# A spectral layer with a gated feed-forward part: who folds which block in the first stage, Newton's steps in three operations, and a new order of the first stage

## The chip, the cores and the metric

The kernel runs on one core of one Trainium2 chip. The metric is the device time of one execution in microseconds (us); smaller is better. Before the change it is 432.95 us, the median of three executions.

## The reference

The input `x` is one sequence of S = 2048 rows of D = 512. A layernorm is followed by a two-dimensional FFT, a filter, and the inverse FFT; a second layernorm is followed by a gated feed-forward part of width F = 1376.

```
def _layernorm(x, axis=-1, eps=1e-5):
    m = jnp.mean(x, axis=axis, keepdims=True)
    v = jnp.var(x, axis=axis, keepdims=True)
    return (x - m) / jnp.sqrt(v + eps)

def _A_ref(x, w_r, w_i):
    X = jnp.fft.rfft2(x, axes=(-2, -1))
    X = X * (w_r + 1j * w_i)
    return jnp.fft.irfft2(X, s=(S, D), axes=(-2, -1))

def _B_ref(x, w_gate, w_up, w_down):
    h = gelu(x @ w_gate, approximate) * (x @ w_up)
    return h @ w_down

h = x + _A_ref(_layernorm(x), w_r, w_i)
out = h + _B_ref(_layernorm(h), w_gate, w_up, w_down)
```

## The kernel before

All transforms are matmuls on TensorE (PE). The first stage takes `x` in 16 blocks of 128 x 512, in the tile `gh`, which arrive in the order of their numbers, blocks 0 and 1 apart and then two at a time. The order of the work on each engine is written out by hand, in the list `START`: a letter is a step, a number its block or group, and each engine gets its instructions in the order of the list. The steps of the first stage are:

- `s` and `g`: statistics of a block. For the blocks in `BY_SCALAR` ScalarE (ACT) does both, with two passes over the block that accumulate a sum (L327, L336); for the others VectorE (DVE) does, with bn_stats and bn_aggr (L330, L338).
- `r`, then `e`, `n`, `o`, `p`: one over the root of the variance for a group of 1, 1, 2, 4, 4 and 4 blocks: a first value by ScalarE (L349), refined by one Newton step that VectorE does in four small operations (L353, L357, L361, L365), with their intermediate values in PSUM.
- `c`: ScalarE scales the block's 128 x 128 of the DFT matrix `mfs` by that factor, into `ms` (L371). It is the moving operand of the block's transforms, so none of them starts ahead of it.
- `f` and `h`: difference and sum of a block's two halves, into `pn` (L391, L395), of one or two blocks at a time. Groups in `ON_VECTOR` are folded by VectorE, the others by GpSimd (POOL).
- `v`: VectorE takes a difference of parts of `pn` into `uv` (L405), from which spectra 2 and 3 are transformed (`b`). Spectra 0 and 1 (`a`) are transformed from `pn` itself, with two matmuls for each that add in PSUM, or, where `u` has added the two parts first into `us` (L412), with one.
- `k` and `l`: ScalarE or VectorE copies a block's spectra from PSUM into `ts` (L433, L436). `w` is TensorE work on the identity ahead of the first data (L204), and `z` clears a part of PSUM.

One matmul in float32 shows as two rows in the profile, so a block's transforms have 12 rows with `pn` (8 for `a`, 4 for `b`) and 8 with `us`.

The second stage has its own list, `SECOND`: `o` transforms over the blocks (L480) and copies the result to `dp` (ScalarE L489, for two tiles partly VectorE L487), `f` is the matmul with `cfs` (L497), the filter on VectorE (L503 to L505) and a sum `z` on GpSimd (L513), `b` the way back (L524, copied at L529), and `p` patches a filter tile (L532). Each `h` takes one more step of work that this stage does not need: the rounding of a weight tile to a high part (ScalarE, L186) and a low part (GpSimd, L187) for the feed-forward matmuls. All later stages have orders of their own, which the change leaves alone.

Of the kernel before, what the change touches and what calls it, by code (L numbers as in the profile page):

```python
# [12 lines left out]
F32 = mybir.dt.float32  # L13
# [3 lines left out]
ALU = mybir.AluOpType  # L17
# [3 lines left out]
P = 128  # L21
NB = 16
# [3 lines left out]
EPS = 1e-5  # L26
# [7 lines left out]
COPIED_BY_VECTOR = (0, 1)  # L34

START = """
s0 f0 h0 f1 h1 v0 s1 f2 g0 r0 h2 f4 e0 n0 g1 o0 p0 s2 s3 r1 e1 n1 g3 o1 s5 c0 p1 g2 r2 e2 g5 v1 n2 s4 h4 w7 o2 p2 c1
g4 f8 a0 v2 c2 b1 s6 g6 s7 g7 a1 b0 b2 c3 r4 f6 k1 s9 e4 s8 n4 g9 a2 o4 k0 p4 b3 c5 s11 g8 s10 a3 a5 c4 f10 g11 h6 v4
g10 a4 s13 e8 s12 c6 h8 b4 r8 c7 b5 n8 a7 s14 s15 k3 o8 v6 k4 a6 p8 h10 b7 u9 k2 b6 v10 u11 c9 c10 v8 f14 a10 h14 b10
f12 g15 c11 a9 c8 g14 k5 g12 b8 k7 g13 e12 r12 b9 h12 n12 o12 p12 u13 u12 a8 k9 a11 k6 v12 b11 c13 f15 u14 h15 a13 u15  # L40
v14 c12 a12 c14 k8 b13 b12 a14 k11 c15 a15 k10 v15 b14 l14 l15 b15 k12 k13 z4 k14 k15
"""

ON_VECTOR = (0, 10, 12, 15)

BY_SCALAR = (0, 2, 4, 6, 11, 14)

YIELDS = ((4, 8, 14), (2, 4, 6, 14))

MEANS = (slice(0, 7, 2), slice(11, 15, 3))  # L50

ROOTS = {0: 1, 1: 1, 2: 2, 4: 4, 8: 4, 12: 4}

# [13 lines left out]
"""  # L67

SECOND = """
h p0 o0.6.0 o0.6.1 o1.0.0 h o1.0.1 h o2.2 p1 f0 f1 h p2 p4 o3.0 o4.2 p5 h f2 p3 h o5.0 f3 o6.2 o7.0 h f4 p9 o8.2 f5 p7  # L70
b0 o9.2 p8 p6 f6 b1 f7 o10.2 h h h b2 f8 p10 o11.2 f9 b3 o12.2 f10 h h b4 p11 f11 p12 o13.2 b5 b6 o14.2 p14 h h p15 h
f12 p13 f13 o15.2 b7 b8 f14 h b9 h f15 b10 b11 h b12 b13 b14.0 b15.0 b14.1 h b15.1
"""
# [76 lines left out]
def kernel(  # L150
# [16 lines left out]
    pe, act, dve, pool = nc.tensor, nc.scalar, nc.vector, nc.gpsimd  # L167
    x3 = x.rearrange("(p b) d -> p b d", b=NB)
    o3 = out[: S // 2].rearrange("(p b) d -> p b d", b=NB // 2)
# [9 lines left out]
    mv = base.tile([P, NB, 2], F32, name="mv")  # L179
# [19 lines left out]
    ps = ctx.enter_context(tc.tile_pool(name="ps", bufs=1, space=PSUM)).tile([P, 8, 512], F32, name="ps")  # L199
# [7 lines left out]
    k3 = ctx.enter_context(tc.tile_pool(name="k3", bufs=1))  # L207
# [7 lines left out]
    def behind(i, ins):  # L215

        how = mybir.DependencyInfo(mybir.DependencyClass.Sync, mybir.DependencyReason.DATA)
        tc.add_manual_dep(i.ins, ins.ins.name, how, reason="leaves the shared port to it")
# [48 lines left out]
    with (  # L267
# [6 lines left out]
        w1 = w1s.enter_context(tc.tile_pool(name="w1", bufs=2))  # L274
        ts = tp.tile([P, NT, 4, 2, NB, 4], F32, name="ts")
        mfs = w1.tile([P, NB, P], F32, name="mfs", bufs=1)
        rs = cp.tile([P, NB], F32, name="rs")
# [45 lines left out]
        def stats(b):  # L323

            if b in BY_SCALAR:
                jk = w1.tile([P, D], F32, name="jk", bufs=2)
# [5 lines left out]
        def merge(b):  # L332

            if b in BY_SCALAR:
                jk = w1.tile([P, D], F32, name="jk", bufs=2)
# [1 line left out]
            else:  # L337
                dve.bn_aggr(mv[:, b], bns[b])  # L338

        tmp = ps[:, 7].rearrange("p (b k) -> p b k", b=NB)  # L340

        def of_root(b):

            bs = slice(b, b + ROOTS[b])
            return rs[:, bs], mv[:, bs, 1], tmp[:, bs, 0], tmp[:, bs, 1]

        def root(b):
            r, var, _, _ = of_root(b)
            act.activation(r, var, AF.Abs_reciprocal_sqrt, bias=eps)  # L349

        def eps_added(b):
            _, var, ve, _ = of_root(b)
            dve.tensor_scalar(ve, var, EPS, None, op0=ALU.add)  # L353

        def newton(b):
            r, _, ve, t = of_root(b)
            dve.scalar_tensor_tensor(t, r, -0.5, ve, op0=ALU.mult, op1=ALU.mult)  # L357

        def newton2(b):
            r, _, _, t = of_root(b)  # L360
            dve.tensor_tensor(t, t, r, op=ALU.mult)  # L361

        def newton3(b):
            r, _, _, t = of_root(b)
            dve.scalar_tensor_tensor(r, t, 1.5, r, op0=ALU.add, op1=ALU.mult)  # L365

        mss, pns, parts = {}, {}, {b: [None] * 4 for b in range(NB)}

# [4 lines left out]
        def halves_of(b):  # L373

            n = group[b][1]
            xv = gh[:, b : b + n].rearrange("p b (e n) -> p b e n", e=2)
            if b not in pns:
                pns[b] = w1.tile([P, 2, 2, 2, P], F32, name="pn", bufs=7)[:, :n]
            return xv, pns[b].rearrange("p b e h n -> p b e (h n)"), dve if b in ON_VECTOR else pool

        def shared(i, eng=dve, yields=False):

            if eng is dve:
                pooled["port"] = i
            elif yields and "port" in pooled:
                behind(i, pooled["port"])
            return i

        def fold(b):
            xv, pv, eng = halves_of(b)  # L390
            shared(eng.tensor_tensor(pv[:, :, 1], xv[:, :, 0], xv[:, :, 1], op=ALU.subtract), eng, b in YIELDS[0])  # L391

        def fold_sum(b):
            xv, pv, eng = halves_of(b)
            shared(eng.tensor_tensor(pv[:, :, 0], xv[:, :, 0], xv[:, :, 1], op=ALU.add), eng, b in YIELDS[1])  # L395
            for i in range(group[b][1]):
# [12 lines left out]
        def sums2(b):  # L409
            pn = pns[group[b][0]][:, b - group[b][0]]  # L410
            us = w1.tile([P, 2, P], F32, name="us", bufs=5)
            shared(dve.tensor_tensor(us, pn[:, :, 0], pn[:, :, 1], op=ALU.add))  # L412
            parts[b][:2] = [[us[:, 0]], [us[:, 1]]]

        def spectrum(b, c):
# [22 lines left out]
        def clear(k):  # L438
# [5 lines left out]
            "s": stats,  # L444
            "g": merge,
            "r": root,
            "e": eps_added,
            "n": newton,
            "o": newton2,
            "p": newton3,  # L450
            "c": scale,
            "f": fold,
            "h": fold_sum,
            "v": fold2,
            "u": sums2,
            "a": lambda b: transform(b, (0, 1)),
            "b": lambda b: transform(b, (2, 3)),
# [5 lines left out]
        with tc.manual_schedule(engines={et.PE, et.Activation, et.DVE, et.Pool}):  # L463
            for op in START.split():
                kept = steps[op[0]](int(op[1:]))
            for b in MEANS:
                dve.tensor_scalar(mv[:, b, 0], m4[:, b], -(D**0.5), None, op0=ALU.mult)
# [66 lines left out]
        with tc.manual_schedule(engines={et.PE, et.Activation, et.DVE, et.Pool}):  # L534
# [8 lines left out]
            for op in SECOND.split():  # L543
                name, *place = op.split(".")
                t = int(name[1:] or 0)
# [324 lines left out]
    def pair(i):  # L870
# [19 lines left out]

        do[f"Q{i}"] = lambda: act.activation(r, mv2[:, bs, 1], AF.Abs_reciprocal_sqrt, bias=eps)
        do[f"E{i}"], do[f"N{i}"] = eps_added, newton
        for h in range(2):
            do[f"R{i}{h}"] = normed(h)
# [484 lines left out]
    with tc.manual_schedule(engines={et.PE, et.Activation, et.DVE, et.Pool}):  # L1379
# [3 lines left out]
        for op in FIRST_HALF.split():  # L1383
            name, _, place = op.partition("@")
# [131 lines left out]
```

## Time and profile before

| | |
|---|---|
| median of 3 executions | 432.95 us (432.94, 432.95, 434.13) |
| the profiled execution | 432.39 us |
| its span in the profile | 430.6 us |
| TensorE busy | 424.2 us (99%) |
| VectorE, ScalarE, GpSimd busy | 310.2 (72%), 258.9 (60%), 318.7 us (74%) |

The time of an execution includes 1.79 us around the span, which runs from the first to the last instruction. Busy times of neighbouring TensorE rows overlap in the profile; the distance between the starts of rows tells the rate. Line numbers are those of the kernel before; the changed kernel's are one to five higher in the parts that matter here.

### The profile page before, as it was taken

The page shows a single profiled execution, that of the slowest core. Times are in us where ns is not written, and L with a number is a line of the kernel's source. Part 1 is how long each engine was busy: PE and PEld are TensorE (multiplying, and loading weights), DVE is VectorE, ACT ScalarE, POOL GpSimd, SP SyncE. Part 2 cuts the span into 40 slices and gives each one's busy share as a digit, 9 for nine tenths or more (in the row PEclk, how much of TensorE's full clock was granted, in tenths as well). Part 3 has the DMA queues.
Part 4 walks back from the last instruction along what each step waited for, and adds up shares of the span by engine and source line. Part 5 has one row for each costly group of instructions (what it writes and reads, how often), then busy time and mean ns, then how long its engine had stood idle before and what let it go on. Part 6 is the DMA issues. An engine that isn't in the chain of part 4 may idle for free.

```text
span 430.6 us, 6599 instructions
## 1 busy us (share of the span) xinstructions
PE 424.2 (99%) x2239; PEld 363.8 (85%) x2239; DVE 310.2 (72%) x593; ACT 258.9 (60%) x524; POOL 318.7 (74%) x345
## 2 busy tenths in 40 slices
PE   8999999999999999999999999999999999999996
PEld 7999999789988888888888888888888888888884
DVE  5979986898725565445866688677777596777785
ACT  6989685799953454346651764466555563566550
POOL 5767897999999998778722684287879777797721
PEclk9999999999999999999999999999999999999999
DMA  8996804210033212203248512520221212100005
GB/s 284 397 414 217 277 30 150 93 50 25 2 123 123 75 49 75 73 0 123 73 109 258 178 69 98 171 68 11 72 72 50 70 29 68 57 24 1 2 1 195
DMA packets 26821, 45.78 MB, mean 106 GB/s; under 512 B 2338, under 2 KB 12066, under 8 KB 26660
## 3 DMA queue, kind: packets, MB, share of 16 engines
q1 hardware_dynamic: 26500, 45.11, 31.7%
q8 instruction: 17, 0.28, 0.3%
q10 hardware_dynamic: 288, 0.26, 0.2%
q14 instruction: 16, 0.13, 0.1%
HBM read 39.06 MB, written 6.30 MB: 105 GB/s over the span
## 4 chain that ended last, share of the span: by engine, by line
PE 97%; DMA 1%; ACT 0%; issue 0%; SPq 0%; DVE 0%; DVEq 0%
PE ps L194 16%; PE ps L193 16%; PE ps L195 16%; PE ps L1262 14%; PE ps L1055 11%; PE ps L425 4%; PE ps L480 3%; PE ps L524 3%; PE ps L591 3%; PE ps L497 3%; PE ps L846 2%; PE ps L1233 1%; DMA gh<-in_x 1%; PE ps L1163 1%; PE ps L624 0%
## 5 line engine op out<-in xcount | busy, mean ns | idle before, releaser
L193 PE MATMUL ps<-cb,gu 128*128 128x512 f32 (+1 forms) x336 | 125.4, 373 | 0.0
L194 PE MATMUL ps<-cb,gu 128*128 128x512 f32 (+1 forms) x336 | 124.9, 372 | 0.0
L195 PE MATMUL ps<-cb,gu 128*128 128x512 f32 (+1 forms) x336 | 124.8, 371 | 0.0
L260 POOL TENSOR_TENSOR gu<-raw,gu 128x768 fp32r<-128x768 f32 (+1 forms) x42 | 61.7, 1483 | 24.0 <-ACT gu L257 21.9
L195 PEld LDWEIGHTS ps<-cb,gu 128*128 128x128 f32 x336 | 63.3, 188 | 11.1
L193 PEld LDWEIGHTS ps<-cb,gu 128*128 128x128 f32 x336 | 63.3, 188 | 10.9
L194 PEld LDWEIGHTS ps<-cb,gu 128*128 128x128 f32 x336 | 63.3, 188 | 10.9
L725 ACT ACTIVATE s<-ps 128x512 f32<-128x512 f32 (+1 forms) x72 | 40.3, 562 | 47.2 <-PE ps L195 42.7
L1262 PE MATMUL ps<-wd,a 128*128 128x512 f32 x264 | 63.1, 389 | 0.0
L1262 PEld LDWEIGHTS ps<-wd,a 128*128 128x128 f32 x264 | 49.5, 188 | 10.3
L734 DVE TENSOR_TENSOR ps<-ps,s 128x512 f32<-128x512 f32 (+1 forms) x48 | 31.1, 651 | 26.0 <-PE ps L195 21.2
L731 ACT ACTIVATE s<-s 128x512 f32<-128x512 f32 (+1 forms) x48 | 28.5, 593 | 27.6 <-DVE s L728 27.4
L1062 DVE TENSOR_TENSOR gh<-ps,gh 128x512 f32<-128x512 f32 x66 | 44.1, 680 | 0.8 <-PE ps L1055 0.8
L728 DVE TENSOR_TENSOR s<-ps,s 128x512 f32<-128x512 f32 (+1 forms) x48 | 30.7, 639 | 5.3 <-PE ps L195 3.9
L257 ACT ACTIVATE gu<-raw 128x768 fp32r<-128x768 f32 (+1 forms) x42 | 28.9, 697 | 9.2 <-DMA raw<-in_wgu 5.9
L1274 DVE TENSOR_TENSOR gh<-ps,gh 128x512 f32<-128x512 f32 x24 | 16.2, 683 | 21.4 <-PE ps L1262 21.4
L728 DVE TENSOR_TENSOR ps<-ps,s 128x512 f32<-128x512 f32 (+1 forms) x24 | 15.6, 651 | 13.2 <-ACT s L725 11.1
L747 DVE TENSOR_TENSOR a<-ps,a 128x512 fp32r<-128x512 f32 (+1 forms) x26 | 15.0, 601 | 11.6 <-ACT a L740 11.2
L572 POOL TENSOR_TENSOR wd<-wdr,wd 128x512 fp32r<-128x512 f32 x12 | 15.6, 1302 | 10.1 <-ACT wd L570 8.8
L513 POOL TENSOR_TENSOR z<-t,t 128x520 f32<-128x520 f32 x15 | 19.5, 1297 | 4.3 <-DVE t L505 3.8
L237 POOL TENSOR_TENSOR raw<-raw 128x256 f32<-128x256 f32 x16 | 11.9, 743 | 14.4 <-DMA raw<-in_wgu 10.9
L489 ACT ACTIVATE dp<-ps 64x512 f32<-64x512 f32 x30 | 17.8, 592 | 5.3 <-PE ps L480 4.9
(188 smaller groups left out, 890.4 us busy)
## 6 DMA issues: line engine op xcount, KB each, us to landing
wt<-in_w SPq DMA_DIRECT2D x16, 520.0 KB, 3.4
raw<-in_wgu SPq DMA_DIRECT2D x32, 256.0 KB, 3.1
out<-gh SPq DMA_DIRECT2D x15, 256.0 KB, 2.0
gh<-in_x SPq DMA_DIRECT2D x7, 512.0 KB, 7.6
row<-in_x SPq DMA_DIRECT2D x12, 256.0 KB, 3.9
wdr<-in_wd SPq DMA_DIRECT2D x12, 256.0 KB, 2.6
mis<-in_wd SPq DMA_DIRECT2D x10, 256.0 KB, 2.6
across<-t SPq DMA_DIRECT2D x8, 256.0 KB, 4.3
```

What stands on the lines that cost most here:

```text
L193: pe.matmul(o, lh, rh, start=(i == 0 and not onto), stop=False, skip_group_check=True)
L194: pe.matmul(o, lh, rl, start=False, stop=False, skip_group_check=True)
L195: last = pe.matmul(o, ll, rh, start=False, stop=(i == n - 1), skip_group_check=True)
L257: by.activation(r[:, 0, m], t[:, m], AF.Copy)
L260: pooled["lo"] = pool.tensor_tensor(r[:, 1, m], t[:, m], r[:, 0, m].bitcast(F32), op=ALU.subtract)
L725: return lambda: act.activation(to, a, AF.Copy)
L728: return lambda: dve.tensor_tensor(to, a, b, op=ALU.add)
L731: return lambda: act.activation(g, g, AF.Gelu_apprx_tanh)
L734: return lambda: dve.tensor_tensor(u, u, g, op=ALU.mult)
L1055: pe.matmul(ps[:, k], w[:, hw], a[ha], start=start and hw + ha == 0, stop=hw == 1, skip_group_check=True)
L1062: by.tensor_tensor(to, o, to, op=ALU.add)
L1262: pe.matmul(o, a[:, ha, i // 4, rows_of], wds[f][:, hw], start=start, stop=stop)
```

## The change

The groups that VectorE folds were blocks 0, 10 and 11, 12 and 13, 15; they become blocks 1, 2 and 3, 12 and 13, 14, 15. GpSimd folds the others. ScalarE takes the statistics of blocks 1, 2, 4, 7, 9, 12 in place of 0, 2, 4, 6, 11, 14. The halves of one more block, block 8, are added ahead of its transforms (`u8`), and that sum for block 14 moves to GpSimd. Newton's step takes three operations in place of four, with the two intermediate values in SBUF tiles (`nw0`, `nw1`) and the first root in PSUM. `START` is written anew, and the first line of `SECOND` has small moves of `o0.6.0` and of some `h`.

```
-ON_VECTOR = (0, 10, 12, 15)
-BY_SCALAR = (0, 2, 4, 6, 11, 14)
-YIELDS = ((4, 8, 14), (2, 4, 6, 14))
-MEANS = (slice(0, 7, 2), slice(11, 15, 3))
+ON_VECTOR = (1, 2, 12, 14, 15)
+BY_SCALAR = (1, 2, 4, 7, 9, 12)
+SUMS_BY_POOL = (14,)
+YIELDS = ((0, 6, 10), (4, 10))
+MEANS = (slice(1, 8, 3), slice(9, 13, 3), slice(2, 3))
...
-h p0 o0.6.0 o0.6.1 o1.0.0 h o1.0.1 h o2.2 p1 f0 f1 h p2 p4 o3.0 o4.2 p5 h f2 p3 h o5.0 f3 o6.2 o7.0 h f4 p9 o8.2 f5 p7
+o0.6.0 h p0 o0.6.1 o1.0.0 h o1.0.1 o2.2 p1 f0 h f1 h p2 p4 o3.0 o4.2 p5 f2 h o5.0 p3 f3 o6.2 o7.0 h f4 p9 h o8.2 f5 p7
...
         def root(b):
-            r, var, _, _ = of_root(b)
+            _, var, r = of_root(b)
             act.activation(r, var, AF.Abs_reciprocal_sqrt, bias=eps)
-        def eps_added(b):
-            dve.tensor_scalar(ve, var, EPS, None, op0=ALU.add)
         def newton(b):
-            dve.scalar_tensor_tensor(t, r, -0.5, ve, op0=ALU.mult, op1=ALU.mult)
+            steps_of[b] = [w1.tile([P, 32], F32, name=f"nw{k}", bufs=2)[:, : ROOTS[b]] for k in range(2)]
+            dve.scalar_tensor_tensor(steps_of[b][0], var, EPS, r, op0=ALU.add, op1=ALU.mult)
         def newton2(b):
-            dve.tensor_tensor(t, t, r, op=ALU.mult)
+            dve.scalar_tensor_tensor(to, t, -0.5, of_root(b)[2], op0=ALU.mult, op1=ALU.mult)
         def newton3(b):
-            dve.scalar_tensor_tensor(r, t, 1.5, r, op0=ALU.add, op1=ALU.mult)
+            dve.scalar_tensor_tensor(to, steps_of[b][1], 1.5, r, op0=ALU.add, op1=ALU.mult)
...
         def sums2(b):
-            shared(dve.tensor_tensor(us, pn[:, :, 0], pn[:, :, 1], op=ALU.add))
+            eng = pool if b in SUMS_BY_POOL else dve
+            shared(eng.tensor_tensor(us, pn[:, :, 0], pn[:, :, 1], op=ALU.add), eng)
```

The beginning of ScalarE's queue for the data, before: the two passes over block 0, its root, the first pass over block 2, the root of block 1, and then the scaling of block 0 (`ms_194`), the second pass over block 2, a root and so on to the scaling of block 1 (`ms_217`).

```order
L327 ACTIVATE jk_158,m4_113<-gh_58 128x512
L336 ACTIVATE jk_172,mv_66<-gh_58,m4_113 128x512
L349 ACTIVATE rs_112<-mv_66,eps_67 128x1
L327 ACTIVATE jk_183,m4_113<-gh_58 128x512
L349 ACTIVATE rs_112<-mv_66,eps_67 128x1
L371 ACTIVATE ms_194<-mfs_111,rs_112 128x128
L336 ACTIVATE jk_197,mv_66<-gh_58,m4_113 128x512
L349 ACTIVATE rs_112<-mv_66,eps_67 128x2
L327 ACTIVATE jk_205,m4_113<-gh_58 128x512
L371 ACTIVATE ms_217<-mfs_111,rs_112 128x128
```

The same place now: the root of block 0, whose statistics VectorE takes, then the passes over blocks 1 and 2 with the root of block 1 between them, the scaling of block 0 (`ms_204`), the first pass over block 4, a root, the second pass over block 4, and the scaling of block 1 (`ms_228`).

```order
L353 ACTIVATE ps_72<-mv_66,eps_67 128x1
L331 ACTIVATE jk_171,m4_113<-gh_58 128x512
L340 ACTIVATE jk_173,mv_66<-gh_58,m4_113 128x512
L331 ACTIVATE jk_181,m4_113<-gh_58 128x512
L353 ACTIVATE ps_72<-mv_66,eps_67 128x1
L340 ACTIVATE jk_200,mv_66<-gh_58,m4_113 128x512
L372 ACTIVATE ms_204<-mfs_111,rs_112 128x128
L331 ACTIVATE jk_208,m4_113<-gh_58 128x512
L353 ACTIVATE ps_72<-mv_66,eps_67 128x2
L340 ACTIVATE jk_223,mv_66<-gh_58,m4_113 128x512
L372 ACTIVATE ms_228<-mfs_111,rs_112 128x128
```

Ahead of the scaling of block 0 stand four passes and two roots now, where before there were three passes and two roots; the passes over block 1 are among them, which need block 1's arrival.

The first transforms on TensorE, before: `a` of block 0, `b` and `a` of block 1, `b` of block 0.

```order
L425 MATMUL ps_72<-ms_194,pn_160 128x128 x4
L425 MATMUL ps_72<-ms_217,uv_202 128x128 x2
L425 MATMUL ps_72<-ms_217,pn_163 128x128 x4
L425 MATMUL ps_72<-ms_194,uv_166 128x128 x2
L425 MATMUL ps_72<-ms_229,uv_227 128x128 x2
```

Now both `a` and `b` of block 0 come first, six matmuls that need only the scaling of block 0.

```order
L427 MATMUL ps_72<-ms_204,pn_168 128x128 x4
L427 MATMUL ps_72<-ms_204,uv_185 128x128 x2
L427 MATMUL ps_72<-ms_228,pn_176 128x128 x4
L427 MATMUL ps_72<-ms_235,uv_226 128x128 x2
L427 MATMUL ps_72<-ms_235,pn_190 128x128 x4
```

The matmuls that need block 1 (`ms_228` now, `ms_217` before) stand behind six matmuls in place of four.

In the second stage ScalarE's queue, before, around the copies `dp`: a patch, two roundings of a weight tile with a patch between them, then six copies.

```order
L532 ACTIVATE wt_150<-wh_449 128x4x2
L186 ACTIVATE gu_97<-raw_135 128x256
L532 ACTIVATE wt_144<-wh_449 128x4x2
L186 ACTIVATE gu_97<-raw_135 128x256
L489 ACTIVATE dp_556<-ps_72 64x512 x2
L489 ACTIVATE dp_575<-ps_72 64x512 x2
L489 ACTIVATE dp_582<-ps_72 64x512 x2
L186 ACTIVATE gu_97<-raw_135 128x256
L532 ACTIVATE wt_514<-wh_449 128x4x2
L489 ACTIVATE dp_607<-ps_72 64x512 x2
```

The same place now:

```order
L533 ACTIVATE wt_150<-wh_456 128x4x2
L190 ACTIVATE gu_97<-raw_135 128x256
L490 ACTIVATE dp_560<-ps_72 64x512 x2
L533 ACTIVATE wt_144<-wh_456 128x4x2
L490 ACTIVATE dp_580<-ps_72 64x512 x2
L490 ACTIVATE dp_587<-ps_72 64x512 x2
L190 ACTIVATE gu_97<-raw_135 128x256
L533 ACTIVATE wt_521<-wh_456 128x4x2
L190 ACTIVATE gu_97<-raw_135 128x256
L490 ACTIVATE dp_614<-ps_72 64x512 x2
```

Of the two roundings ahead of the fourth tile's copy (`dp_556` before, `dp_560` now) one has moved behind the sixth's, where two now stand ahead of `dp_614`, the copy that was `dp_607`.

## Rows read from the trace of the kernel before

**Rows 1.** The page: span, busy time by engine, shares of the last chain.

```profile
span 430.6 us, 6599 instructions
...
PE 424.2 (99%) x2239; PEld 363.8 (85%) x2239; DVE 310.2 (72%) x593; ACT 258.9 (60%) x524; POOL 318.7 (74%) x345
...
PE 97%; DMA 1%; ACT 0%; issue 0%; SPq 0%; DVE 0%; DVEq 0%
```

**Rows 2.** Busy time by stretch: first stage from its first wait on; late stages.

```profile
10.00:28.50 18.50, 18.48 (x160) 18.25 (x161) 17.86 (x53) 17.05 (x46) 11.90 (x11) 1.00 1.03 404
...
124.00:411.00 287.00, 287.00 (x1268) 237.43 (x1267) 197.52 (x342) 153.17 (x272) 213.06 (x210) 1.00 0.25 75
```

**Rows 3.** TensorE's timeline: start, time, instructions, idle time ahead and its releaser.

```profile
1.37 7.05 PE L204 MATMUL ps<-ident 128*128 128x128 f32 x42 [1.37 <-POOL ident masks.py:199]
8.26 1.06 PE L425 MATMUL ps<-ms,pn 128*128 128x128 f32 x8
10.02 0.71 PE L425 MATMUL ps<-ms,uv 128*128 128x128 f32 x4 [0.70 <-ACT ms L371]
...
26.60 1.22 PE L425 MATMUL ps<-ms,us 128*128 128x128 f32 x8
27.66 1.06 PE L425 MATMUL ps<-ms,uv 128*128 128x128 f32 x8
28.55 3.13 PE L480 MATMUL ps<-dfs,ts 128*128 128x128 f32 x24
...
37.88 2.25 PE L480 MATMUL ps<-dfs,ts 128*128 128x128 f32 x16
```

**Rows 4.** The first stage's instructions by tile: the matmuls on sums of halves.

```profile
L425 PE MATMUL ps<-ms,us 128*128 128x128 f32 x24 | 3.5, 278 | 0.0
```

**Rows 5.** ScalarE's timeline in the first stage.

```profile
6.82 0.63 ACT L327 ACTIVATE jk<-gh 128x512 f32<-128x512 f32 x1 [0.43 <-DMA gh<-in_x]
...
7.45 0.28 ACT L349 ACTIVATE rs<-mv,eps 128x1 f32<-128x1 f32 x1
7.64 0.39 ACT L371 ACTIVATE ms<-mfs,rs 128x128 f32<-128x128 f32 x1
7.93 0.71 ACT L336 ACTIVATE jk<-gh,m 128x512 f32<-128x512 f32 x1
...
9.57 0.39 ACT L371 ACTIVATE ms<-mfs,rs 128x128 f32<-128x128 f32 x1
9.87 0.71 ACT L336 ACTIVATE jk<-gh,m 128x512 f32<-128x512 f32 x1
...
10.57 0.39 ACT L371 ACTIVATE ms<-mfs,rs 128x128 f32<-128x128 f32 x1
```

**Rows 6.** GpSimd's timeline: the first fold of block 1.

```profile
5.60 0.73 POOL L391 TENSOR_TENSOR pn<-gh 128x256 f32<-128x256 f32 x1 [4.28 <-DMA gh<-in_x]
```

**Rows 7.** VectorE's timeline in the first stage.

```profile
4.42 0.42 DVE L391 TENSOR_TENSOR pn<-gh 128x256 f32<-128x256 f32 x1 [3.55 <-DMA gh<-in_x]
4.76 0.42 DVE L395 TENSOR_TENSOR pn<-gh 128x256 f32<-128x256 f32 x1
...
5.56 0.68 DVE L330 BATCH_NORM_STATS2 bn<-gh 128x6 f32<-128x512 f32 x1
...
9.05 0.17 DVE L338 BATCH_NORM_AGGREGATE mv<-bn 128x2 f32<-128x6 f32 x1
9.14 0.62 DVE L405 TENSOR_TENSOR uv<-pn 128x256 f32<-128x256 f32 x1
...
10.14 1.29 DVE L405 TENSOR_TENSOR uv<-pn 128x512 f32<-128x512 f32 x1
...
15.51 0.68 DVE L405 TENSOR_TENSOR uv<-pn 128x512 f32<-128x512 f32 x1
```

**Rows 8.** ScalarE's timeline around the copies `dp` of the second stage.

```profile
37.30 0.40 ACT L186 ACTIVATE gu<-raw 128x256 fp32r<-128x256 f32 x1
37.73 3.72 ACT L489 ACTIVATE dp<-ps 64x512 f32<-64x512 f32 x6
```

More of the change, by code (lines that the diff above doesn't have):

```diff
@@ L36 @@
 START = """
[L37 to L41, printed above, removed]
-"""
-ON_VECTOR = (0, 10, 12, 15)
-BY_SCALAR = (0, 2, 4, 6, 11, 14)
-YIELDS = ((4, 8, 14), (2, 4, 6, 14))
-MEANS = (slice(0, 7, 2), slice(11, 15, 3))
+w7 s0 g0 f0 r0 s1 g1 h0 f1 n0 s2 h1 o0 v0 f4 p0 f2 r1 h2 n1 s3 o1 g2 h4 p1 c0 f6 s4 g3 r2 a0 h6 s5 n2 o2 g4 p2 v2 c1
+b0 s6 g6 c2 a1 g5 s7 v1 g7 b2 s8 r4 c3 n4 o4 p4 k0 a2 b1 c5 b3 c4 v4 f10 a3 c7 v6 s11 g11 s9 h10 a4 s10 k3 k2 s13 g8
+g9 g10 r8 f14 g13 b5 s14 f8 b4 a7 n8 o8 u11 s12 p8 g14 h8 a5 b7 c6 b6 g12 c10 a6 s15 g15 h14 v10 k4 c9 r12 c11 v8 a10
+k1 b11 n12 o12 b10 b9 k7 p12 c14 a11 c8 u9 a9 c13 k6 c12 f12 b8 h12 u8 u14 a14 k5 k10 k9 a8 k8 u12 a12 c15 k11 u13 v12
+f15 a13 h15 b12 k12 v14 u15 b13 k13 v15 b14 a15 k14 l14 b15 l15 z4 k15
+"""
+ON_VECTOR = (1, 2, 12, 14, 15)
+BY_SCALAR = (1, 2, 4, 7, 9, 12)
+SUMMED = ()
+SUMS_BY_POOL = (14,)
+YIELDS = ((0, 6, 10), (4, 10))
+MEANS = (slice(1, 8, 3), slice(9, 13, 3), slice(2, 3))
 ROOTS = {0: 1, 1: 1, 2: 2, 4: 4, 8: 4, 12: 4}
@@ L338, in merge @@
                 dve.bn_aggr(mv[:, b], bns[b])
-        tmp = ps[:, 7].rearrange("p (b k) -> p b k", b=NB)
+        roots, steps_of = ps[:, 7].rearrange("p (b k) -> p b k", b=NB)[:, :, 0], {}
         def of_root(b):
             bs = slice(b, b + ROOTS[b])
-            return rs[:, bs], mv[:, bs, 1], tmp[:, bs, 0], tmp[:, bs, 1]
+            return rs[:, bs], mv[:, bs, 1], roots[:, bs]
         def root(b):
-            r, var, _, _ = of_root(b)
+            _, var, r = of_root(b)
             act.activation(r, var, AF.Abs_reciprocal_sqrt, bias=eps)
-        def eps_added(b):
-            _, var, ve, _ = of_root(b)
-            dve.tensor_scalar(ve, var, EPS, None, op0=ALU.add)
         def newton(b):
-            r, _, ve, t = of_root(b)
-            dve.scalar_tensor_tensor(t, r, -0.5, ve, op0=ALU.mult, op1=ALU.mult)
+            _, var, r = of_root(b)
+            steps_of[b] = [w1.tile([P, 32], F32, name=f"nw{k}", bufs=2)[:, : ROOTS[b]] for k in range(2)]
+            dve.scalar_tensor_tensor(steps_of[b][0], var, EPS, r, op0=ALU.add, op1=ALU.mult)
         def newton2(b):
-            r, _, _, t = of_root(b)
-            dve.tensor_tensor(t, t, r, op=ALU.mult)
+            t, to = steps_of[b]
+            dve.scalar_tensor_tensor(to, t, -0.5, of_root(b)[2], op0=ALU.mult, op1=ALU.mult)
         def newton3(b):
-            r, _, _, t = of_root(b)
-            dve.scalar_tensor_tensor(r, t, 1.5, r, op0=ALU.add, op1=ALU.mult)
+            to, _, r = of_root(b)
+            dve.scalar_tensor_tensor(to, steps_of[b][1], 1.5, r, op0=ALU.add, op1=ALU.mult)
         mss, pns, parts = {}, {}, {b: [None] * 4 for b in range(NB)}
@@ L446 @@
             "r": root,
-            "e": eps_added,
             "n": newton,
```

## The prediction, on record before the changed kernel's time was known

> **What bounds the kernel now.** I read the page first. TensorE is busy for 424.2 of 430.6 us, and 97% of the last chain is TensorE's own work [rows 1]. So the time changes by what TensorE does less or more, and by what it waits less or more, and by nothing else. The view by stretches then says where a wait could be mended. In the first stage TensorE is busy 18.48 of 18.50 us and so, nearly, is VectorE with 17.86; late, from 124 to 411 us, TensorE is busy 287.00 of 287.00 [rows 2]. That has two consequences. Whatever the first two stages gain or lose is passed on to the end one for one, since behind them lies no idle time that could take it up. And busy time counts a short wait between overlapping rows as work, so the rate must be read from the starts of rows in TensorE's timeline.
>
> There, eight dense rows take 0.89 us (27.66 to 28.55), 0.111 each [rows 3]. The first eight rows of data start at 8.26, right behind 42 warm-up rows that began at 1.37. They would be through at 8.26 + 0.89 = 9.15, but the next start is at 10.02, with ScalarE's scaling L371 named: **0.87 us lost in front**. From 10.02 to the second stage's first row at 28.55 there are 160 rows; dense they are 20 x 0.89 = 17.80, and they took 18.53: **0.73 us lost in small pieces**. One is seen at 26.60, where eight rows on sums of halves take 1.06 until the next start, 0.17 too long. In the second stage 24 rows that would take 23 x 0.111 + 0.28 = 2.83 (a row's own length, from 1.06 for eight) took 3.13 at its start, 0.30 lost; and 16 rows at 37.88 took 2.25 for 15 x 0.111 + 0.28 = 1.95, another 0.30.
>
> **The change part by part.**
>
> *Matmuls.* Sums of halves for six blocks make 24 rows now [rows 4]. Block 8 joins them: its spectra 0 and 1 take 4 rows in place of 8. TensorE does 4 rows less: 4 x 0.111 = **-0.45 us**. Nothing else on TensorE is added or removed; the warm-up's 42 rows stay ahead of the first transform.
>
> *The front.* Warm-up ends at 8.26 as before, and what decides is ScalarE's queue, as in before. Its prices are from one start to the next: a first pass 0.63 (6.82 to 7.45), a root 0.19 (7.45 to 7.64), a scaling 0.29 (7.64 to 7.93) and 0.39 until its end, a second pass 0.70 (9.87 to 10.57) [rows 5]. The scaling that ended the wait was at 9.57; 9.57 + 0.39 = 9.96, and TensorE started 0.06 later. In the new queue the passes over block 1 can't start before that block is there, at 5.60, where GpSimd's first fold of it starts after waiting for it [rows 6]. From there: pass 5.60, second pass 6.23, pass over block 2 6.93 (its data were there at 6.82 [rows 5]), root 7.56, second pass 7.75, scaling of block 0 at 8.45, done at 8.84, first transform at **8.90 in place of 8.26**. The root of block 0 is no obstacle: its data are there at 4.42, bn_stats takes 0.68, and the root and three steps still have 3.3 us until 8.45 [rows 7]. Then 12 rows of block 0 follow, to 8.90 + 1.33 = 10.23. Meanwhile ScalarE does a pass at 8.74, a root at 9.37, a pass at 9.56, and the scaling of block 1 from 10.26 to 10.65; block 1's transforms start at 10.71, 0.48 late. So 0.64 + 0.48 = 1.12 are lost in place of 0.87, **+0.25**; I take **+0.3**, since the second pass over block 1 needs the sum of the first and can't follow as closely as the row says (an estimate, 0.05). Bounds: -0.87, if the whole front loss vanished, which the queue's prices exclude down to about 0, and +0.6, if ScalarE's four passes each came 0.1 later.
>
> *Newton's steps.* Six groups lose one operation each. On VectorE such an operation takes 0.09 from start to start (9.05 to 9.14) [rows 7], so VectorE gains about 0.5 us. None of it is on TensorE's path in front, since the scaling waits behind ScalarE's passes and not on the root. It is VectorE's room, counted next.
>
> *VectorE's and GpSimd's folds.* VectorE now folds seven blocks where it folded six. A block's fold is two operations of 0.34 from start to start (4.42 to 4.76 [rows 7]): +0.7, against -0.5 from Newton's steps; the sums of halves stay at six. Its 17.86 of 18.50 become about 18.05, still under the stage's length. So it keeps up, as barely as before, and I expect the small losses to remain of the same kind. How large they are the trace can't say; the order only shows that in the last four blocks every fold by VectorE stands directly ahead of the matmuls that use it. Between nothing (0.73 gained) and double (0.73 lost) I take somewhat less than before, 0.43 in place of 0.73, **-0.3**, because 0.17 of it lay at 26.60, where sums of halves came last, and one of these sums has gone to GpSimd, which is busy only 11.90 of 18.50 [rows 2].
>
> What speaks against moving folds to VectorE stands in the same timeline. A `uv` of 256 took 0.62 at 9.14 while GpSimd folded, and an operation of 256 with its inputs in SBUF took 0.42 at 4.42 while GpSimd still waited; of 512 they took 1.29 at 10.14 and 0.68 at 15.51 [rows 7]. So a fold can wait up to 0.61 for GpSimd. That is a rule of the Trainium skill too ("SBUF — State Buffer", section "Who interferes with whom"): a VectorE instruction with two inputs in SBUF and a GpSimd instruction that reads SBUF exclude each other, and the later one blocks until the first is through. The trace agrees, with these numbers. The sum doesn't need the rule: GpSimd folds ten blocks before and nine now, so meetings should be about as many, and I price them at nothing, with the rival below for the other case.
>
> *The start of the second stage.* `o0.6.0` ahead of a rounding changes nothing on TensorE; its first rows wait for the last copies out of PSUM, 0.30 before. In the new list the copies of ScalarE's last two blocks stand in another order and VectorE's copies come between: **+0.1**, bounds -0.3 and +0.3.
>
> *The second stage.* Before, a rounding of 0.40 at 37.30 stands directly ahead of the copies at 37.73 [rows 8], and the matmuls that wait on them are among the 0.30 lost at 37.88. This rounding has moved away, but the order shows it two copies on, where two roundings now stand ahead of one tile's copy. A stall goes and its like comes: **0**, bounds -0.3 and +0.3. On GpSimd one low part of 0.7 goes with each.
>
> *Later stages*: nothing is changed, and the shift is carried.
>
> The sum: -0.45 + 0.3 - 0.3 + 0.1 + 0 = **-0.35 us**. The profiled execution would go from 432.39 (430.6 of span and 1.79 around it) to about 432.05. It was 0.56 below the median, so the median goes from 432.95 to **432.6**, 0.1% less. A measurement of this kernel can tell about 0.3%, 1.3 us, from no change, as the three runs from 432.94 to 434.13 suggest.
>
> **The rivals.**
>
> *Faster than can be missed.* The waits vanish rather than move: the front's 0.87 of before becomes 0.3, the small pieces 0.73 become 0.1, the stall at 37.88 goes without a successor: -0.45 - 0.57 - 0.63 - 0.3 = -1.95, about **431.0**. For it: all of these are waits, not work. Against it: ScalarE's queue, whose prices put the first transform at 8.90. Chance 0.10.
>
> *TensorE's clock.* The 42 warm-up rows took 7.05; dense it would be 41 x 0.111 + 0.28 = 4.83, so some 20 of them ran at twice the distance, and this at the start of the program, after 1.37 us of idling [rows 3]. If the two gaps of 0.64 and 0.48 brought this slow start back, the next 20 rows would cost 20 x 0.111 = 2.2 us more: -0.35 + 2.2, about **434.8**, slower. It decides as soon as a gap of the new front is long enough. Against it: a gap of 0.70 stood in before at 10.02, with the granted clock at 1.00 from 10 us on [rows 2], its upper level of 2.4 GHz. Chance 0.04.
>
> *VectorE becomes the bound.* With its room of 0.64, reduced to 0.45, two more waits of 0.61 for GpSimd than before would make it late by 0.77 in the stage's last blocks, where each of its folds has matmuls directly behind; four would make it 2.0. With the small losses of before not reduced either, that is -0.45 + 0.3 + 0.1 + 0.77 = +0.7 or +1.95, about **433.7** or **434.9**. For it: VectorE now folds beside GpSimd right at the front. Against: GpSimd is idle for 6.6 of 18.5 us. Chance 0.10, of which 0.04 beyond 0.3%.
>
> *Nothing to be seen*, because the front costs what the matmuls save: between 432.6 and 433.3, inside the likeliest case's range.
>
> **How the numbers follow.** The forecast has 0.76, the faster rival 0.10, the clock 0.04, VectorE 0.10. The forecast's own range, from the terms' bounds taken together without all falling on one side, is 431.8 to 433.5. For 8 in 10 with the rivals on both sides I give 431.4 to 434.0. Faster by over 0.3% (below 431.65): the faster rival's 0.10 and 0.03 of the forecast's edge, 0.13. Slower by over 0.3% (above 434.25): 0.04 for the clock, 0.04 for VectorE, 0.08. The same: 0.79.
>
> **What would show it.** 164 rows of transforms in place of 168; the first at about 8.9, a gap of some 0.5 ahead of block 1's near 10.7; the second stage's first row 0.3 to 0.5 earlier than 28.55; one stall of about 0.3 in the second stage some 4 us later than 37.88; the same TensorE busy time from 124 us on. Wrong it would be if the first gap were under 0.3 or over 1, if the starts of rows behind a gap were 0.22 apart, or if the last folds of VectorE came after 27.7, where TensorE needs them.

## The result, and the profile after

The changed kernel takes 433.7 us (median of 22 executions, 433.17 to 436.08), against 432.91 us before (22 executions beside them, 432.5 to 434.13): a ratio of 1.0022, with a 95% interval of 1.0014 to 1.0030. It is slower by about 0.8 us, small but clear of the noise. The forecast was 0.35 us faster, with a range of 431.4 to 434.0 and a chance of 0.79 for no difference over 0.3%. The time lies within that range, but the sign was wrong.

The profiled execution of the changed kernel took 434.84 us, 1.1 above its own median, and that of the kernel before 432.39, 0.5 under its median. So the difference of the two traces, 2.5 us, is three times the one to be explained, and part of the work was to tell what belongs to most executions and what to these two.

First the page and the view by stretches (columns as in [rows 1, 2]).

```profile
span 433.1 us, 6577 instructions
...
PE 425.1 (98%) x2235; PEld 363.7 (84%) x2235; DVE 312.1 (72%) x590; ACT 258.4 (60%) x524; POOL 317.3 (73%) x344
```

```profile
10.00:28.50 18.50, 17.39 (x148) 16.71 (x147) 17.98 (x47) 15.87 (x45) 10.95 (x10) 1.00 1.03 401
...
124.00:411.00 287.00, 286.71 (x1264) 236.81 (x1263) 195.99 (x340) 151.97 (x270) 214.14 (x210) 1.00 0.25 77
```

TensorE has four rows less, as said. It waits for over 1 us in the first stage, and for the first time it also shows idle time between 124 and 411 us, where before it was busy 287.00 of 287.00 [rows 2]. Where, its timeline says:

```profile
1.37 7.30 PE L208 MATMUL ps<-ident 128*128 128x128 f32 x42 [1.37 <-POOL ident masks.py:199]
9.04 1.13 PE L427 MATMUL ps<-ms,pn 128*128 128x128 f32 x8 [0.37 <-ACT ms L372]
10.00 0.61 PE L427 MATMUL ps<-ms,uv 128*128 128x128 f32 x4
10.74 1.16 PE L427 MATMUL ps<-ms,pn 128*128 128x128 f32 x8
...
19.33 1.06 PE L427 MATMUL ps<-ms,pn 128*128 128x128 f32 x8
21.14 1.13 PE L427 MATMUL ps<-ms,pn 128*128 128x128 f32 x8 [0.75 <-ACT ms L372]
22.50 1.76 PE L427 MATMUL ps<-ms,uv 128*128 128x128 f32 x12 [0.23 <-DVE uv L406]
...
29.21 0.61 PE L427 MATMUL ps<-ms,uv 128*128 128x128 f32 x4
30.04 2.94 PE L481 MATMUL ps<-dfs,ts 128*128 128x128 f32 x24 [0.22 <-DVE ps L442]
...
39.18 1.95 PE L481 MATMUL ps<-dfs,ts 128*128 128x128 f32 x16
...
44.87 1.16 PE L481 MATMUL ps<-dfs,ts 128*128 128x128 f32 x8 [0.23 <-ACT dp L490]
```

The front is as forecast: first transform at 9.04 (8.90 forecast), block 1's at 10.74 (10.71). New is 19.33 to 22.50: 16 rows that would take 1.78 take 3.17. The second stage begins at 30.04, 1.49 later than in [rows 3]. The stall of 0.30 at 37.88 is gone (16 rows at 39.18 take 1.95) and its like stands at 44.87, as forecast.

The cause of the gap at 21.14 is on VectorE and GpSimd. Their timelines, and ScalarE's scaling that waits for them:

```profile
17.45 1.60 DVE L392 TENSOR_TENSOR pn<-gh 128x256 f32<-128x256 f32 x1 [0.21 <-DMA gh<-in_x]
...
20.41 0.15 DVE L366 SCALAR_TENSOR_TENSOR rs<-nw,ps 128x4 f32<-128x4 f32 x1
```

```profile
16.22 1.30 POOL L396 TENSOR_TENSOR pn<-gh 128x512 f32<-128x512 f32 x1
17.46 1.31 POOL L392 TENSOR_TENSOR pn<-gh 128x512 f32<-128x512 f32 x1
```

```profile
20.59 0.40 ACT L372 ACTIVATE ms<-mfs,rs 128x128 f32<-128x128 f32 x1 [1.35 <-DVE rs L366]
```

VectorE's first fold of block 14 became ready when the block arrived, at 17.45, as one GpSimd fold ended and 10 ns ahead of the start of the next. It took 1.60 us, 1.2 more than the 0.42 of [rows 7], and ended when GpSimd's 1.31 us and its own time were over. Behind it in VectorE's queue stood the Newton steps of blocks 8 to 11, for these the scaling waited, and for the scaling TensorE.

The later loss is another matter. Here is the chain of waits of the changed kernel from 196 to 207 us (start, time, what):

```profile
196.34 0.33 SPq L234
196.67 0.05 issue
196.72 4.64 DMA raw<-in_wgu
...
201.51 0.75 POOL raw L241
...
203.16 0.75 POOL raw L247
203.93 0.03 ACT gu L261
...
205.29 0.74 ACT gu L261
206.03 0.49 ACT s L726
206.52 0.04 issue
206.56 0.50 PE ps L197
```

A load of a weight tile (`raw`) takes 4.64 us after its issue; GpSimd waits, so ScalarE's rounding waits, and a copy out of PSUM that stands behind it in ScalarE's queue, so TensorE. Nothing in the code of this stage had been touched. Here is the end of that wait on GpSimd in the changed kernel, and then in the kernel before, where GpSimd waited 0.21 us for the same load (1.15 in a second trace, which still lost nothing here):

```profile
201.51 0.74 POOL L241 TENSOR_TENSOR raw<-raw 128x256 f32<-128x256 f32 x1 [2.40 <-DMA raw<-in_wgu]
```

```profile
198.71 0.74 POOL L237 TENSOR_TENSOR raw<-raw 128x256 f32<-128x256 f32 x1 [0.21 <-DMA raw<-in_wgu]
```

### The profile page after: what moved, and what is told of

The parts are those of the page before. It is cut to its first block, busy times and chain, and to the rows that moved or that the text cites. A ratio compares the mean times of both kernels' runs of the same rounds, so it can differ in the third digit from the quotient of the medians.

```text
span 433.1 us, 6577 instructions
## 1 busy us (share of the span) xinstructions
PE 425.1 (98%) x2235; PEld 363.7 (84%) x2235; DVE 312.1 (72%) x590; ACT 258.4 (60%) x524; POOL 317.3 (73%) x344
## 4 chain that ended last, share of the span: by engine, by line
PE 87%; DMA 5%; ACT 3%; DVE 2%; POOL 2%; issue 1%; SPq 0%; DVEq 0%; POOLq 0%; ACTq 0%
PE ps L197 15%; PE ps L198 15%; PE ps L199 15%; PE ps L1263 14%; PE ps L1056 11%; DMA gh<-in_x 4%; PE ps L592 3%; PE ps L525 3%; PE ps L481 3%; PE ps L498 3%; PE ps L847 2%; PE ps L1164 1%; DMA raw<-in_wgu 1%; PE ps L1234 1%; ACT ts L435 1%; POOL gu L264 1%
```

## The experiments

Each kernel ran on a chip beside the kernel before. "Loss near 204" is worked out from TensorE's timelines: how much the shift against the first trace of the kernel before grows between the rows of 175 and of 246 us. The first four were to find what belongs to most executions.

**e1: the changed kernel again.** 

> The changed kernel as it is, for a second trace. In its profiled execution blocks 6 to 15 of x arrived 0.4 to 0.5 us later than in that of the kernel before, and VectorE's first fold of block 14 began at 17.45, together with a fold by GpSimd, and took 1.60 us in place of some 0.41. Theory A (the wait of VectorE for GpSimd): the fold of block 14 is long (over 1.2 us) again, in most executions, and the time is 0.6 to 1.0 us above the kernel before. Rival B (late arrival alone, by chance): with x in time the fold takes 0.4 to 0.6 us and the second stage's first row is at about 28.3, earlier than the 28.55 of before.

Measured: 433.75 us (433.33 to 436.69, 12 executions), ratio 1.0027 (1.0012 to 1.0042). The profiled execution took 435.06, and its fold of block 14 was as long (VectorE's timeline):

```profile
17.72 1.62 DVE L392 TENSOR_TENSOR pn<-gh 128x256 f32<-128x256 f32 x1 [0.36 <-DMA gh<-in_x]
```

But 9 of the 12 executions lie between 433.33 and 433.85. Both traces are of long executions, so they don't show that most executions have the long fold, which theory A expected.

**e2: GpSimd waits for VectorE's fold of block 14.** 

> GpSimd's first fold of blocks 8 and 9 waits until VectorE's first fold of block 14, which stands ahead of it in the list, is done. Nothing else is changed. Theory A: VectorE's fold takes 0.4 to 0.5 us, GpSimd's comes up to 0.9 later, the second stage begins at 28.5 to 28.9 in place of 30.04, and the time is 0.6 to 1.0 us less than the changed kernel's, at or 0.3 under the kernel before (432.6 to 432.9). Rival C (the front and the new order cost it, not this wait): the time stays within 0.2 us of the changed kernel's, as GpSimd is only made later.

```
-YIELDS = ((0, 6, 10), (4, 10))
+YIELDS = ((0, 6, 8, 10), (4, 10))
```

Measured: 433.77 us (433.29 to 434.3, 11 executions), ratio 1.0018 (1.0009 to 1.0026). The fold is now short, and the second stage begins at 29.56:

```profile
17.80 0.42 DVE L392 TENSOR_TENSOR pn<-gh 128x256 f32<-128x256 f32 x1 [0.20 <-DMA gh<-in_x]
```

No execution was over 434.3. But the median stayed: the wait of VectorE makes the long executions, not the 0.8 us of most. The loss near 204 is 1.01 in this trace.

**e3: the matrix's second part loaded after x.** 

> The second part of the DFT matrix (512 KB, needed from block 8 on) is loaded after all of x in place of between blocks 8 and 10, so blocks 10 to 15 arrive about 1.3 us earlier. Theory A, with the arrival as the trigger: block 14 is there when VectorE comes to its fold at about 17.0, while GpSimd is in the middle of a fold, so VectorE waits 0.1 to 0.5 us and not 1.2; the second stage begins at about 28.3 and the time is 0.8 to 1.2 us less than the changed kernel's. Rival C: the arrival of x doesn't matter, since the front has lost the time already: within 0.2 us of the changed kernel. Rival D: the matrix comes too late for block 8's scaling: slower.

```
         for b in range(6, NB, 2):
             load_x(b, b + 2)
-            if b == 8:
-                load_m(8, NB)
+        load_m(8, NB)
```

Measured: 433.44 us (432.85 to 433.94, 11 executions), ratio 1.0010 (1.0001 to 1.0018). The fold took 0.66 us at 16.86, and the second stage began at 28.47, 0.08 earlier than in the kernel before, yet the profiled execution took 432.91 for 432.39: it lost 0.59 near 204. So the first stage was mended and the kernel still slow, which sent me to that loss.

**e4: the second stage's old first line.** 

> The changed kernel with the first line of the second stage's list as it was before. Theory A: the second stage's order is worth nothing or little, 0.0 to -0.2 us against the changed kernel, and the time stays 0.5 to 0.9 above the kernel before. Rival E (the new first line of the second stage costs the time): the time falls by 0.5 us or more, to that of the kernel before.

The edit is the diff's line of `SECOND` taken back. Measured: 433.12 us (432.95 to 433.44, and one of 435.88), ratio 1.0009 (0.9996 to 1.0021). Its trace gains 0.19 in the second stage, and loses 0.59 near 204. The median moved by 0.6, more than the trace's 0.19: by the median the rival came true, by the trace it did not, and the record doesn't reconcile the two.

**e5: the kernel before again.** 

> The kernel before, unchanged, for a second trace of it. All five traces of changed kernels lose 0.6 to 1.0 us between 175 and 246 us (two or three waits of matmuls on rounded weights, near 204 and 214 us), and the first trace of the kernel before loses nothing there; its time, 432.39, is 0.6 under its own median. Theory G: that loss belongs to most executions of either kernel, and this trace shows it, with a time near 433.0. Rival H: it comes from the change, and this trace has none.

Measured: 432.99 us, one execution. H holds: no loss near 204 (shift 0.65 at 175 us and 0.63 at 246). But the second stage begins late here too:

```profile
29.23 3.13 PE L480 MATMUL ps<-dfs,ts 128*128 128x128 f32 x24
```

That is 0.68 later than in [rows 3]. In the first trace of the kernel before `x` came early (block 14 was there at 16.98, here at 17.52), so its 28.55 is a poor mark for other executions.

**e6: the kernel before with the second stage's new line.** 

> The kernel before with only the first line of the second stage's list as in the change. Theory S (the second stage's new order costs): +0.2 us by the trace (rows of the second stage lose 0.2 against the old order), up to +0.6 by the difference of the medians of the changed kernel with the new and with the old line (433.75 and 433.12). Rival A (the second stage is worth nothing): within 0.15 us of the kernel before.

Measured: 433.33 us (432.78 to 433.96, 11 executions), ratio 1.0008 (0.9999 to 1.0017). Its trace loses 0.18 in the second stage, as e4's gained 0.19, and nothing near 204. That is about +0.2 for the new line; the interval still holds zero.

**e7: Newton in three operations alone.** 

> The kernel before with only Newton's step in three operations in place of four; order and owners as before. As predicted: VectorE has some 0.4 us less to do in the first stage, none of it on TensorE's path in front, so the time stays within 0.2 us of the kernel before. Rival: VectorE is the bound of the first stage, and it gains 0.2 to 0.5 us.

The four operations of the kernel before are replaced by the three of the diff, and the six `e` taken out of `START`. Measured: 432.78 us (432.6 to 433.34, 11 executions), ratio 0.9999 (0.9990 to 1.0007): nothing, as predicted.

**e8: late matrix and old second line.** 

> The changed kernel with both: the second part of the DFT matrix loaded after all of x, and the old first line of the second stage's list. If the losses are the wait of VectorE for GpSimd at block 14 and the second stage's order, and each is mended by its edit alone (medians 433.44 and 433.12 in place of 433.75), both together give 432.6 to 432.9, at or under the kernel before, and no execution above 434.5. Rival: the edits mend the same loss, and the time is 433.1, as with the old line alone.

Measured: 433.5 us (432.74 to 433.89, 11 executions), ratio 1.0008 (0.9999 to 1.0017). By the medians both edits together did not reach the kernel before, though the interval just holds it. Its trace loses 0.96 near 204.

So a loss near 204 stood in all six traces with the new first stage (0.59 to 1.01) and in none of the four with the old one (-0.02 to 0.10). What differs there is seen in the DMA queues. The view of DMA by queue, from 197.7 to 199.2 us of the changed kernel (packets, MB, share):

```profile
q8 instruction: 1, 0.02, 3.9%
```

and from 193 to 194.5 us of the kernel before's second trace:

```profile
q8 instruction: 1, 0.02, 4.1%
```

This is a load of 16 KB of program; that it is TensorE's is read from its moving with four TensorE rows more or less (e9 and e11 below). There are 17 of them in an execution; late they come about every 29 us. In the changed kernel it lies within the transfer of the weight tile, with 1013 matmul rows of TensorE still to come; in the kernel before 1027 and 1029 rows are still to come (two traces), so it lies 14 to 16 rows, over 3 us, earlier in the program, in another transfer. A transfer is done in 16 parts, and the trace has the time at which each of them completed. The table has, in us, the last two of the weight tile's second half and of that other transfer, a down-projection tile, which is issued ahead of the weight tile with one transfer between them:

```
kernel (trace)      load begins  other transfer     weight tile's 2nd half   loss near 204
before              193.97       195.36  196.47     198.51  198.55           0.00
before again (e5)   194.03       195.92  196.54     199.40  199.55          -0.02
changed             198.77       197.03  197.10     200.19  201.36           0.68
old second (e4)     196.78       195.44  195.44     198.27  199.48           0.59
late matrix, old
  second (e8)       197.08       195.66  195.68     198.66  200.11           0.96
pad (e9)            196.22       198.14  199.25     202.10  202.14           0.34
old second, pad
  (e10)             193.58       195.54  196.23     198.51  198.56           0.01
before less (e11)   197.33       195.68  195.72     198.79  199.93           0.56
late matrix, old
  second, pad (e12) 193.41       195.36  196.31     198.14  198.34          -0.02
```

Whichever of the two transfers the load falls into has one part out of 16 that comes 0.6 to 1.5 us behind the others. With the load at 194 us that is a transfer whose late part costs TensorE nothing; with the load some 3 us later it is the weight tile. The seven traces left out of the table agree: the weight tile's last part is 1.25 to 1.43 behind the one before it in e1, e2 and e3, and at most 0.06 in e6, e7, e13 and e14, which have the load at 193.39 to 194.13. (e9's whole stage is 2.8 us late, so its 196.22 is as early in the program as e10's 193.58; its 0.34 stands without a late part.) Now the position was moved by itself, both ways.

**e9: two warm-up matmuls more.** 

> The changed kernel with two warm-up matmuls (4 rows, 8 instructions) more, in the gap of 0.6 us ahead of its first transform, so that TensorE's program is again as long as before up to every later matmul. Theory I (instruction loading): in all six traces with the new first stage a 16 KB instruction load of TensorE's (0.95 us on one DMA engine) falls at 196.8 to 198.8 us into the load of a weight tile, whose last of 16 parts lands 1.2 to 1.4 us behind the others, and TensorE loses 0.6 to 1.0 us there; in the four traces with the old first stage it falls at 194.0, on a transfer that nobody waits for. Then this kernel has no such loss and is 0.5 to 0.9 us faster than the changed kernel (433.7), at 432.8 to 433.2. Rival: the loss has another cause in the new first stage, and the time stays at 433.7 or rises by up to 0.45 (the four rows).

```
-w7 s0 g0 f0 r0
+w9 s0 g0 f0 r0
```

Measured: 433.01 us (432.58 to 436.65, 12 executions), ratio 1.0013 (0.9997 to 1.0030). The median is 0.7 under the changed kernel's, from work that was *added*, and 7 of the 12 executions are under 433.17, the fastest of the changed kernel's 34. The profiled execution was a long one again, 435.64 us, now with two folds by GpSimd ahead of VectorE's, in VectorE's and GpSimd's timelines:

```profile
17.76 2.90 DVE L392 TENSOR_TENSOR pn<-gh 128x256 f32<-128x256 f32 x1 [0.35 <-DMA gh<-in_x]
```

```profile
17.81 1.31 POOL L392 TENSOR_TENSOR pn<-gh 128x512 f32<-128x512 f32 x1
19.07 1.30 POOL L396 TENSOR_TENSOR pn<-gh 128x512 f32<-128x512 f32 x1
```

**e10: the same with the old second line.** 

> The same with the second stage's old first line as well. Theory I and S: the losses add, 433.12 of the old line alone less 0.5 to 0.6, so 432.5 to 432.7, at or 0.4 under the kernel before. Rival: one loss only, 433.1.

Measured: 432.91 us (432.58 to 434.42, 12 executions), ratio 1.0002 (0.9991 to 1.0013). That is 0.1 under e9 and at the kernel before, above the 432.5 to 432.7 expected; the 0.4 under the kernel before that the losses' sum allowed didn't come. GpSimd's wait for the weight tile's load, which was 2.40 in the changed kernel, is 0.46 here:

```profile
198.72 0.74 POOL L241 TENSOR_TENSOR raw<-raw 128x256 f32<-128x256 f32 x1 [0.46 <-DMA raw<-in_wgu]
```

**e11: the kernel before with two warm-up matmuls less.** 

> The kernel before with two warm-up matmuls (4 rows, 8 instructions) less; its first transform waits for ScalarE's scaling at about 8.0, so it can start no later than before. Theory I: the instruction load moves into the weight tile's transfer as in the changed kernel, 0.5 to 1.0 us are lost near 204 us, and the time is 433.4 to 433.9. Rival (the loss belongs to the new first stage): 432.8 to 433.0, as the kernel before or 0.1 less.

```
-s4 h4 w7 o2
+s4 h4 w5 o2
```

Measured: 433.77 us (433.26 to 435.02, 11 executions), ratio 1.0019 (1.0010 to 1.0028): with nothing of the change but four rows less, the kernel before becomes as slow as the changed one. The shorter warm-up is not what costs it: with block 14 there at 17.37 the second stage began at 28.84, no later than e6's 29.14 with block 14 at 17.44, and 0.56 are lost near 204. GpSimd's timeline shows the same wait:

```profile
200.08 0.75 POOL L237 TENSOR_TENSOR raw<-raw 128x256 f32<-128x256 f32 x1 [2.33 <-DMA raw<-in_wgu]
```

**e12: two matmuls more, old second line, late matrix.** 

> The changed kernel with the warm-up's two matmuls, the old second line and the late load of the DFT matrix's second part. Theory A with I and S: no loss near 204, none in the second stage, and VectorE's fold of block 14 never waits for a whole fold by GpSimd: 432.2 to 432.6, and no execution over 433.5. Rival (the early arrival of blocks 10 to 15 is worth nothing): the same as with the old line and the two matmuls.

Measured: 432.42 us (432.27 to 432.95, 11 executions), ratio 0.9991 (0.9983 to 1.0000), the fastest kernel of the study. No execution was over 433, and the trace lost nothing near 204.

**e13: the kernel before with the late matrix.** 

> The kernel before with the second part of the DFT matrix loaded after all of x, and nothing else. In the traces of the old first stage the second stage's first row follows the arrival of x (28.55, 29.23 and 29.46 with x later from one to the next). Theory B (x's arrival bounds the old first stage as well): blocks 10 to 15 come 1.3 us earlier and the time falls by 0.3 to 0.6 us, to 432.4 to 432.7, so the gain of the kernel with late masks, old second line and two matmuls more is this load's and not the change's. Rival (the new first stage is what gains once its losses are mended): within 0.2 us of the kernel before.

Measured: 432.73 us (432.39 to 433.34, 11 executions), ratio 0.9996 (0.9987 to 1.0005). That is 0.12 under the kernel before beside it (432.85), which the rival allows, and 0.03 above theory B's range; the interval holds both. Against e12's 0.9991 the intervals overlap, so whether the new first stage adds to the early arrival is not told apart.

**e14: two matmuls more, and GpSimd waits at block 14.** 

> The changed kernel with two warm-up matmuls more, and GpSimd's first fold of blocks 8 and 9 made to wait for VectorE's first fold of block 14. Theory A for the slow executions (in 5 of 12 executions with the two matmuls alone the time is 433.3 to 436.7, and its trace shows a fold of 2.90 us): no execution over 434, a fold of 0.4 to 0.5 us, and a median of 432.9 to 433.3. Rival: the slow executions have another cause and stay.

Measured: 433.02 us (432.73 to 433.54, 11 executions), ratio 1.0005 (0.9996 to 1.0014). The fold is short, in VectorE's timeline:

```profile
17.18 0.48 DVE L392 TENSOR_TENSOR pn<-gh 128x256 f32<-128x256 f32 x1
```

Over 434.5 us were 6 of 34 executions of the changed kernel and 2 of 12 with the two matmuls; with the fold kept clear (by the wait in e2 and e14, by the earlier arrival in e3, e8 and e12) it is 0 of 55. Of the new first stage with neither, e4 had one (435.88) in 11 and e10 none in 12; and e11, with the old first stage, had one of 435.02 that this fold can't explain and that no trace shows. All three traces of such executions show the fold at 1.60, 1.62 and 2.90 us, and the traces of shorter ones at 0.42 to 0.66.

## Why the prediction was wrong, by its own steps

**The step that failed: "Later stages: nothing is changed, and the shift is carried."** It rested on 287.00 of 287.00 busy, which showed that no wait was there, not that none could come. The four rows taken off TensorE (the one certain gain, -0.45) also shortened its program, by 8 instructions (a matmul and a weight load for each row), and moved a program load into a weight tile's transfer. That costs 0.59 to 1.01 us by six traces, and 0.7 by medians (433.7 to 433.01, e9). It is shown both ways: four rows back in mend it, four rows out of the kernel before (433.04 beside it, 433.77 with them out, e11) make it. The gain in front and the loss at 204 are one and the same edit.

The Trainium skill tells of these loads ("Runtime: NRT & Kernel Launch", section "Instruction fetch mechanics"): each engine's sequencer fetches its program in 16 KiB blocks of 256 instructions by a DMA queue of its own, at a cost that is mostly hidden. The size agrees with the loads of q8 in the trace, 16,384 bytes. By the 256 of that section of the Trainium skill an estimate for 17 loads is 4352 instructions, and only TensorE, with 2235 matmul rows and as many weight loads, has that many. The cost is hidden from TensorE's own queue here as well, as far as the chain tells: it names no wait of TensorE's for instructions. What isn't hidden is the data transfer that the load meets.

**The second stage** (0 forecast, bounds -0.3 to 0.3): within bounds. The stall went from 37.88 and came back two copies on, as said; the new line costs about 0.2 more than the old (+0.18 in e6, -0.19 in e4, by traces).

**The front** (+0.3): right, also in its two starts. Of the lost time by the same place, 24 rows done at 12.18 are 2.67 dense from 8.26, so 1.25 were lost; before, 28 rows by 12.35 lost 0.97 (12.35 is the start of the next rows there). The difference is 0.28.

**Small waits of the first stage** (-0.3) and the sum of the stage: not seen, and the second step that failed. By pairs of traces in which block 14 arrived at nearly the same time (the completion of its load, then the second stage's first row), the new first stage against the old:

```
changed (e4)  17.05 28.82    before        16.98 28.55
changed (e10) 17.35 28.92    before (e6)   17.44 29.14
changed (e2)  17.78 29.56    before (e7)   17.79 29.46
```

It is -0.2 to +0.3, with 0.45 of matmuls gone and -0.35 forecast up to there. Three pairs are few, and the arrival is not all that sets this start: in e13 block 14 was there at 15.99 and the second stage began at 28.71. But e10, with the loss near 204 mended and the old second line, says the same by its median: 432.91 against 433.04, where -0.35 is only just within the interval. The start of the second stage took part of it: 0.83 from 29.21 to 30.04 for four rows that are 0.45 dense, 0.38 lost, in every trace with the new order, and 0.19 of it given back in the rows that follow (2.94 for 3.13). I forecast +0.1 for it.

**The rival "VectorE becomes the bound"** (0.10): its mechanism is real and its frequency was off. I priced the wait of a fold at up to 0.61, from the longest in the trace. In three traces a fold that became ready as GpSimd changed from one fold to the next waited for a whole one, 1.2 us, or for two, 2.5. Whether it does hangs on the arrival of block 14 in that execution, which a single trace doesn't tell. It makes the long executions, 6 of 34 (two of them were traced), not the median. The page of the Trainium skill that the prediction named ("SBUF — State Buffer", section "Who interferes with whom") lets whoever issues first go first. Here VectorE was ready first by the profile's starts, by 10 to 50 ns in three traces, and went second or third; in e10's trace, ready 60 ns ahead, it went first (0.43 us, and GpSimd's fold took 1.54). So in these traces the order of the starts didn't decide it.

**Newton's steps** (nothing on the path): right, e7. **TensorE's clock** (0.04): didn't come; the granted clock is 1.00 through the gaps.

Open: why the load moved by 14 to 16 rows, over 3 us, where 8 instructions are 4 rows; why e9 loses 0.34 near 204 without a late part; and why e4's median is 0.6 under the changed kernel's with the loss near 204 still in its trace and only 0.19 gained in the second stage.

## What to carry to other kernels

A change of TensorE's instruction count moved a later program load against the data transfers here, and may do so elsewhere; before a difference of some tenths of a per cent is put down to the edit itself, put the count back with idle-time matmuls and time it again. Where an engine is 100% busy in a late stage, ask what slack the loads behind it have, not whether it waits now. Take two traces of each kernel before comparing one with the other: two traces of the same kernel before began the second stage 0.68 us apart, nearly the whole difference to be explained.

## What the runs showed of the hardware

- In the table above a load of 16,384 bytes of TensorE's program took 0.93 to 1.44 us, and one of the 16 parts of the data transfer that it met came 0.6 to 1.5 us behind the other 15; the tile waits for the last.
- A VectorE fold of 0.42 us waited 1.2 us for one GpSimd fold (two traces), and 2.5 us for two in a row (one trace, e9): there two GpSimd instructions in a row went ahead of it.
- The arrival of block 14 varied from 16.98 to 17.79 us between executions with the same order of loads, and in the kernel before, e6, e7 and e11 the second stage's start with it, from 28.55 to 29.46.
